# Per-head transposes of an attention gradient: from TensorE to the DMA crossbar, and the 1/rowsum multiply from GpSimd to VectorE

## Chip, cores, metric

One core of one Trainium2 chip (trn2). The metric is the device time of one execution in microseconds; lower is better. Between the executions of one kernel the time moves by some tenths of a per cent, in pin_both by 0.8%.

## The reference

The kernel computes the output and eight gradients of a block with a residual: `x + attention(layernorm(x)) * silu(gated_mlp(B_x))`. What matters here is the attention and its backward pass: 32 heads, 2048 queries and 2048 keys, head size 128, model width 576, bf16.

```python
def _A_ref(x, k_cache, v_cache, wq, wo):
    B, Sq, D = x.shape                       # 1, 2048, 576
    H, Dh = 32, 128
    q = (x @ wq).reshape(B, Sq, H, Dh).transpose(0, 2, 1, 3)
    scores = jnp.einsum("bhqd,bhkd->bhqk", q, k_cache) * (Dh ** -0.5)
    p = _softmax(scores, axis=-1)
    o = jnp.einsum("bhqk,bhkd->bhqd", p, v_cache)
    return o.transpose(0, 2, 1, 3).reshape(B, Sq, H * Dh) @ wo
# ... x + s * g, then jax.vjp of the whole for x, K, V, wq, wo and the three MLP weights
```

## The kernel before

Each head takes 32 steps, which I call slots. Slots 0 to 15 are pass 1, one row tile of 128 queries each: scores `sp` (TensorE), `exp` into a slab `Pq` (ScalarE), row sums and their reciprocals `rinv_all` (VectorE), and a transpose of the whole slab, `PT<-Pq`, by the DMA crossbar (the path on which a DMA transposes while it copies), 512 KB each. Five slots later `acc<-Vn,PT` uses PT. Slots 16 to 31 are pass 2: `dp`, then `Pq<-t,Pq` and `Pq<-dp,..` (VectorE), another crossbar transpose `dST<-Pq`, and five slots later `acc<-Kn,dST`. Between them lie the partial products for dV (`acc<-dOn,Pq`) and dK (`acc<-Qn,Pq`), which are staged in `kvo` and stored. So the crossbar already moves 32 x 512 KB per head, all issued from SyncE (SP).

Each head also needs its small operands in two layouts. Before the change TensorE makes them, in blocks of 128x128, and VectorE or ScalarE copies them out of PSUM, the memory that TensorE writes its results to:

```python
def pe_transpose_blocks(src_fn, lo, hi, dst_fn, eng):
    for g in range(lo, hi, 8):
        n = min(8, hi - g)
        pt = acc_tile(bf)                    # one of 4 PSUM buffers shared with every acc
        for j in range(n):
            nc.tensor.transpose(pt[:, j, :], src_fn(g + j), ident[:])
        alt.copy(dst_fn(g, n), pt[:, :n, :], eng=eng)

def prep_kt(hs):                             # prep_vt, prep_qn, prep_don, prep_wot: likewise
    KTv = hs.KT[:].rearrange("p (t q) -> p t q", q=P)
    pe_transpose_blocks(lambda j: hs.Kn[:, j, :], 0, NT, lambda g, n: KTv[:, g:g + n, :], "s")
# ...
def transpose_slab(hs, qt, name):            # the crossbar transposes of PT and dST
    T = wpt.tile([P, NT, P], bf, name=name, tag="PT")
    nc.sync.dma_start_transpose(T[:], hs.slabs[qt][:])
    return T
```

GpSimd multiplies dO and Q by 1/rowsum, and negates `delta`:

```python
def scale_don(hs, qt):
    nc.gpsimd.tensor_scalar(hs.dOn[:, qt, :], hs.dOn[:, qt, :], hs.rinv_all[:, qt:qt + 1], None, op0=ALU.mult)
# tail1, after acc<-Vn,PT of one row tile:
    nc.vector.scalar_tensor_tensor(junk[:], op_[:, 0, :], 1.0, hs.dOn[:, qt, :], op0=ALU.mult, op1=ALU.mult,
                                   accum_out=hs.delta[:, qt:qt + 1])
    nc.gpsimd.tensor_scalar(hs.negdelta[:, qt:qt + 1], hs.delta[:, qt:qt + 1], -1.0, None, op0=ALU.mult)
def post1(hs):                               # once, as pass 2 starts
    nc.gpsimd.tensor_scalar(hs.rsc[:], hs.rinv_all[:], SCALE, None, op0=ALU.mult)
    nc.gpsimd.tensor_tensor(hs.Qn[:], hs.Qn[:], hs.rsc[:].unsqueeze(2).to_broadcast([P, NT, P]), op=ALU.mult)
# main2:
    nc.scalar.activation(t[:], dp[:], AF.Identity, bias=hs.negdelta[:, qt:qt + 1], scale=1.0)
    nc.vector.tensor_tensor(Pq[:, hsl], t[:], Pq[:, hsl], op=ALU.mult)
# Partial.step, second half of dK or dV:
    fo_ = stg.tile([P, 4, P], bf, name="kvo")            # stg: two buffers
    nc.vector.tensor_tensor(fo_[...], self.tile[...], self.part[...], op=ALU.add)
    nc.gpsimd.dma_start(self.out_dram..., fo_[...])
# plan(h): which slot each piece is put at, in the program text (b1: slot 0 of the head, b2: slot 16)
    put(pl + q(skew + 3), NT * P, lambda: prep_kt(hd()))              # slot 24 of the head before
    put(b1 + q(sc + 1), nb * P, lambda sc=sc: prep_don(hd(), sc))     # slots 1..4
    put(b1 + qt + 1, 0, lambda qt=qt: scale_don(hd(), qt))
    put(b1 + q(NSC + 2), NT * P, lambda: prep_vt(hd()))               # slot 6
    put(b1 + q(NTH + 2), NT * P, lambda: prep_qn(hd()))               # slot 10
    put(b2 + 1, 0, lambda: post1(hd()))
```

## Time and profile before

| | before |
|---|---|
| time, median | 5353.21 us (3 executions) |
| attention stretch | 535 to 3731 us of the span |
| one head (mean of heads 4 to 27) | 100.2 us |

The first view is the top of the page of before: busy time and instructions of each engine, the DMA queues (packets, MB, share of 16 engines), and the chain that ended last by engine. The queue called hardware_dynamic is SyncE's, with the crossbar; software_dynamic is GpSimd's.

```profile
PE 5067.8 (95%) x54343; PEld 3653.5 (68%) x55220; DVE 2540.5 (48%) x5776; ACT 2649.6 (50%) x4710; POOL 1415.3 (26%) x2361
...
q1 hardware_dynamic: 2637890, 764.83, 71.7%
q0 software_dynamic: 83296, 280.64, 15.7%
...
PE 82%; issue 4%; DMA 2%; DVE 2%; SPq 2%; ACT 1%; POOL 1%; ACTq 0%; DVEq 0%; POOLq 0%
```

The second view takes 1000 to 3000 us of before (attention only): busy us of PE, PEld, DVE, ACT and POOL with instruction counts, then the granted clock, the DMA share and GB/s.

```profile
1000.00:3000.00 2000.00, 1932.53 (x24756) 1548.01 (x25153) 1167.44 (x2615) 1331.67 (x2256) 636.90 (x1097) 1.00 1.04 204
```

TensorE is busy 97% of this stretch. The DMA engines' share is 1.04. It can pass 1 because it adds up packets that overlap on one engine.

The waits of before, in us in total, times, and longest us:

```profile
ACT t L590 <- POOL negdelta L572: 175.8, 95, 3.0
PE dp L583 <- DVE Pq L586: 75.3, 78, 5.5
DVE kvo L627 <- DMA out_dram<-kvo: 23.6, 14, 6.1
```

For PT or dST, the crossbar's slab transposes, TensorE doesn't wait at all in before. One group of the page (busy us, mean ns of one, then idle time before it with its releaser):

```profile
L591 DVE TENSOR_TENSOR Pq<-t,Pq 128x1024 bf16<-128x1024 bf16 x512 | 422.6, 825 | 369.9 <-ACT t L590 366.4
```

The timeline of before, around one start of pass 2 (start us, us, engine, line, operation, tiles, and in brackets the idle time before it with its releaser):

```profile
1588.29 0.69 DVE L591 TENSOR_TENSOR Pq<-t,Pq 128x1024 bf16<-128x1024 bf16 x1 [0.69 <-ACT t L590]
...
1589.17 3.61 POOL L577 TENSOR_TENSOR Qn<-Qn,rsc 128x2048 bf16<-128x2048 bf16 x1
...
1590.49 2.84 DVE L591 TENSOR_TENSOR Pq<-t,Pq 128x1024 bf16<-128x1024 bf16 x1
...
1592.76 0.65 POOL L572 TENSOR_SCALAR negdelta<-delta 128x1 f32<-128x1 f32 x1
...
1594.79 0.38 PE L583 MATMUL dp<-VT,dOT 128*128 128x512 bf16 x1 [1.54 <-DVE Pq L586]
```

The same VectorE instruction takes 0.69 us alone and 2.84 us beside GpSimd's large multiply; then TensorE idles 1.54 us for it. The Trainium skill, page "SBUF — State Buffer", section "SBUF: two separate sides", describes a shared port pair of VectorE and GpSimd that is "an exclusive lock, not a bandwidth split". The 2.15 us of extra time agrees with that: the VectorE instruction ends at 1593.33 us, 0.55 us after GpSimd's.

### The profile page before, as it was taken

What the parts mean: (1) busy time and instruction counts of PE and PEld (TensorE: products, weight loads), DVE (VectorE), ACT (ScalarE), POOL (GpSimd) and SP (SyncE); (2) the same over time, 40 slices, a digit from 0 to 9 for tenths busy, and PEclk for the clock granted to TensorE, in tenths of its full rate; (3) what the DMA queues carried; (4) which work ended last, traced back from release to release, by engine and by line L of the source; (5) the groups of instructions that cost most, each with busy time, mean ns of one, the idle gap of its engine ahead of it and who ended that gap; (6) DMA issues with size and microseconds to landing.
All of it is one profiled execution on the core that took longest, in us unless ns stands there. A gap on an engine that the chain in (4) does not pass through costs nothing.

```text
span 5343.5 us, 129930 instructions
## 1 busy us (share of the span) xinstructions
PE 5067.8 (95%) x54343; PEld 3653.5 (68%) x55220; DVE 2540.5 (48%) x5776; ACT 2649.6 (50%) x4710; POOL 1415.3 (26%) x2361
## 2 busy tenths in 40 slices
PE   8899999999999999999999999999689999898999
PEld 3345777777777777777777777777457777544454
DVE  5644565566566566556566566566233333210011
ACT  7641766666666666666666666666222222100000
POOL 2122332332332332332332332332112232111000
PEclk9999999999999999999999999999899999999999
DMA  8767999999999999999999999999754455764875
GB/s 301 281 210 169 208 201 197 201 204 208 196 206 208 204 200 207 196 204 209 200 204 207 200 205 208 203 203 201 219 178 165 168 185 180 208 198 125 164 148 109
DMA packets 2721787, 1053.94 MB, mean 197 GB/s; under 512 B 2521937, under 2 KB 2642386, under 8 KB 2719138
## 3 DMA queue, kind: packets, MB, share of 16 engines
q1 hardware_dynamic: 2637890, 764.83, 71.7%
q0 software_dynamic: 83296, 280.64, 15.7%
q8 instruction: 433, 7.09, 0.6%
q14 instruction: 168, 1.38, 0.1%
HBM read 213.91 MB, written 201.00 MB: 78 GB/s over the span
## 4 chain that ended last, share of the span: by engine, by line
PE 82%; issue 4%; DMA 2%; DVE 2%; SPq 2%; ACT 1%; POOL 1%; ACTq 0%; DVEq 0%; POOLq 0%
PE acc L618 16%; PE acc L558 15%; PE acc L913 7%; PE sp L514 7%; PE accw L841 6%; PE dp L583 6%; PE acc L223 5%; PE dh L818 3%; PE accq L881 3%; PE acc L872 2%; PE acct L176 2%; PE acc L439 2%; PE accd L830 2%; PE acc L780 2%; DMA out_dram<-kvo 2%
## 5 line engine op out<-in xcount | busy, mean ns | idle before, releaser
L532 ACT ACTIVATE Pq<-sp 128x1024 bf16<-128x1024 f32 x1024 | 1047.0, 1023 | 307.8 <-PE sp L514 193.6
L618 PEld LDWEIGHTS <-Pq 128*128 128x128 bf16 x16384 | 1002.2, 98 | 240.4 <-issue 0.6
L590 ACT ACTIVATE t<-dp,negdelta 128x1024 bf16<-128x1024 f32 x512 | 571.1, 1115 | 283.3 <-POOL negdelta L572 175.8
L586 DVE SCALAR_TENSOR_TENSOR Pq<-dp,delta,Pq 128x1024 bf16<-128x1024 f32 x512 | 655.1, 1279 | 34.0 <-PE acc L558 32.0
L583 PE MATMUL dp<-VT,dOT 128*128 128x512 bf16 x1728 | 540.4, 379 | 75.8 <-DVE Pq L586 75.3
L591 DVE TENSOR_TENSOR Pq<-t,Pq 128x1024 bf16<-128x1024 bf16 x512 | 422.6, 825 | 369.9 <-ACT t L590 366.4
L558 PEld LDWEIGHTS <-PT 128*128 128x128 bf16 x8192 | 501.9, 98 | 121.6 <-issue 0.3
L618 PE MATMUL acc<-dOn,Pq 128*128 128x128 bf16 x8192 | 546.2, 219 | 10.1
L558 PE MATMUL acc<-Kn,dST 128*128 128x128 bf16 x8192 | 551.4, 219 | 3.6
L558 PE MATMUL acc<-Vn,PT 128*128 128x128 bf16 x8192 | 546.7, 219 | 7.0
L514 PE MATMUL sp<-KT,QT 128*128 128x512 bf16 x1762 | 547.1, 379 | 1.9 <-ACT Pq L532 1.9
L618 PE MATMUL acc<-Qn,Pq 128*128 128x128 bf16 x8192 | 541.5, 219 | 3.4
L558 PEld LDWEIGHTS <-dST 128*128 128x128 bf16 x8192 | 492.5, 98 | 61.2
L547 POOL TENSOR_SCALAR dOn<-dOn,rinv_all 128x128 bf16<-128x128 bf16 x512 | 312.6, 611 | 612.3 <-DVE rinv_all L520 495.4
L600 ACT ACTIVATE dq_n<-acc,rsc 128x128 bf16<-128x128 f32 x512 | 188.1, 367 | 326.1 <-PE acc L558 326.1
L841 PEld LDWEIGHTS <-xn_all 128*128 128x128 bf16 (+1 forms) x2880 | 281.5, 100 | 40.3 <-issue 11.1
L50 DVE TENSOR_SCALAR o_n<-acc,rinv_all 128x128 bf16<-128x128 f32 x352 | 123.5, 351 | 278.4 <-PE acc L558 277.7
L628 POOL DMA_DIRECT2D out_dram<-kvo x256 | 148.4, 580 | 394.8 <-DVE kvo L627 392.4
L583 PEld LDWEIGHTS <-dOT 128*128 128x128 bf16 x2048 | 164.9, 98 | 108.0 <-issue 85.8
L922 ACT ACTIVATE dxn<-acc 128x512 f32<-128x512 f32 (+1 forms) x32 | 12.7, 411 | 421.2 <-PE acc L913 421.2
L519 DVE TENSOR_REDUCE rs_all<-rsp 128x1 f32<-128x2 f32 x512 | 78.2, 153 | 291.9 <-ACT Pq L532 289.6
L552 POOL DMA_DIRECT2D dq_d<-dq_n x128 | 97.9, 765 | 441.4 <-ACT dq_n L600 431.0
(188 smaller groups left out, 7257.5 us busy)
## 6 DMA issues: line engine op xcount, KB each, us to landing
out_dram<-kvo POOLq DMA_DIRECT2D x256, 128.0 KB, 4.3
h_d<-h_row POOLq DMA_DIRECT2D x48, 384.0 KB, 4.1
a_d<-a_row POOLq DMA_DIRECT2D x48, 384.0 KB, 3.9
b_d<-b_row POOLq DMA_DIRECT2D x48, 384.0 KB, 4.6
a_blk<-a_d SPq DMA_DIRECT2D x18, 1024.0 KB, 5.8
b_blk<-b_d SPq DMA_DIRECT2D x18, 1024.0 KB, 18.7
h_blk<-h_d POOLq DMA_DIRECT2D x18, 1024.0 KB, 11.6
du_d<-du_blk POOLq DMA_DIRECT2D x18, 1024.0 KB, 9.1
```

Of the source, the lines that this page charges most:

```text
L223: nc.tensor.matmul(av[:, :CH], lhsT=w[:kk, i, :], rhs=srcT[:kk, i, cs], start=(i == 0), stop=(i == DT - 1))
L514: nc.tensor.matmul(sp[:, c * CH:(c + 1) * CH], lhsT=hs.QT[:, qt * P:(qt + 1) * P], rhs=hs.KT[:, hf * HW_ + c * CH: hf * HW_ + (c + 1) * CH ...
L532: nc.scalar.activation(Pq[:, hsl], sp[:], AF.Exp, scale=SCALE, accum_out=hs.rsp[:, hf:hf + 1])
L547: nc.gpsimd.tensor_scalar(hs.dOn[:, qt, :], hs.dOn[:, qt, :], hs.rinv_all[:, qt:qt + 1], None, op0=ALU.mult)
L558: nc.tensor.matmul(hs.acc[:, 0, :], lhsT=T[:, kt, :], rhs=rhs[:, kt, :], start=(kt == 0), stop=(kt == NT - 1))
L583: nc.tensor.matmul(dp[:, c * CH:(c + 1) * CH], lhsT=hs.dOT[:, qt * P:(qt + 1) * P], rhs=hs.VT[:, hf * HW_ + c * CH: hf * HW_ + (c + 1) * C ...
L586: nc.vector.scalar_tensor_tensor(Pq[:, hsl], dp[:], hs.delta[:, qt:qt + 1], Pq[:, hsl], op0=ALU.subtract, op1=ALU.mult)
L590: nc.scalar.activation(t[:], dp[:], AF.Identity, bias=hs.negdelta[:, qt:qt + 1], scale=1.0)
L591: nc.vector.tensor_tensor(Pq[:, hsl], t[:], Pq[:, hsl], op=ALU.mult)
L618: nc.tensor.matmul(self.tile[:, j, :], lhsT=self.slabs[qt][:, kt * P:(kt + 1) * P], rhs=self.rhs[:, qt, :], start=(qt == self.lo), stop=(q ...
L841: nc.tensor.matmul(acc[:kd, :], lhsT=xn_all[:, st, d0:d0 + kd], rhs=blk_[:, st, :], start=(st == 0), stop=(st == NT - 1))
L913: nc.tensor.matmul(accs[sl][j][:, :nn], lhsT=ch[:, kk, sl * P:(sl + 1) * P], rhs=wT[:, k0 + kk, n0:n0 + nn], start=(kidx == 0), stop=(kidx ...
```

## The change

Its intent: the transposes need no TensorE time if the crossbar does them; and if VectorE multiplies by 1/rowsum in one row tile at a time, GpSimd holds no port against it. The core of the diff (loads, padding of `wo_h` to five full blocks, and signatures are cut):

```diff
 def prep_kt(hs):
-    pe_transpose_blocks(lambda j: hs.Kn[:, j, :], 0, NT, lambda g, n: KTv[:, g:g + n, :], "s")
+    nc.sync.dma_start_transpose(hs.KT[:].rearrange("p (t q) -> p t q", q=P), hs.Kn[:].rearrange("p t d -> p (t d)"))
 # prep_vt and prep_wot likewise
 def prep_don(hs, sc):
-    pe_transpose_blocks(lambda j: hs.dOT[:, j * P:(j + 1) * P], sc * nb, (sc + 1) * nb, ...)
+    nc.sync.dma_start_transpose(hs.dOn[:, sc * nb:(sc + 1) * nb, :], hs.dOT[:, sc * CH:(sc + 1) * CH])
 def prep_qn(hs):
-    pe_transpose_blocks(lambda j: hs.QT[:, j * P:(j + 1) * P], 0, NT, ...)
+    nc.sync.dma_start_transpose(hs.Qn[:], hs.QT[:])
 ...
 def scale_don(hs, qt):
-    nc.gpsimd.tensor_scalar(hs.dOn[:, qt, :], ...)
+    nc.vector.tensor_scalar(hs.dOn[:, qt, :], ...)
+def scale_qn(hs, qt):
+    nc.vector.tensor_scalar(hs.Qn[:, qt, :], hs.Qn[:, qt, :], hs.rinv_all[:, qt:qt + 1], None, op0=ALU.mult)
 ...
-    nc.vector.scalar_tensor_tensor(junk[:], op_[:, 0, :], 1.0, hs.dOn[:, qt, :], ..., accum_out=hs.delta[:, qt:qt + 1])
-    nc.gpsimd.tensor_scalar(hs.negdelta[:, qt:qt + 1], hs.delta[:, qt:qt + 1], -1.0, None, op0=ALU.mult)
+    nc.vector.scalar_tensor_tensor(junk[:], op_[:, 0, :], -1.0, hs.dOn[:, qt, :], ..., accum_out=hs.negdelta[:, qt:qt + 1])
 def post1(hs):
-    nc.gpsimd.tensor_scalar(hs.rsc[:], hs.rinv_all[:], SCALE, None, op0=ALU.mult)
-    nc.gpsimd.tensor_tensor(hs.Qn[:], hs.Qn[:], hs.rsc[:].unsqueeze(2).to_broadcast([P, NT, P]), op=ALU.mult)
+    nc.vector.tensor_scalar(hs.rsc[:], hs.rinv_all[:], SCALE, None, op0=ALU.mult)
 # main2: the last half adds negdelta where it subtracted delta
 # Partial: SCALE is now the factor of the dK copies (scalar_tensor_tensor with factor, mult and add)
 ...
-    put(b1 + qt + 1, 0, lambda qt=qt: scale_don(hd(), qt))
+    put(b1 + max(qt + 1, q(4 + qt // nb)), 0, lambda qt=qt: scale_don(hd(), qt))
-    put(b1 + q(NTH + 2), NT * P, lambda: prep_qn(hd()))
+    put(b1 + q(NTH + 1), 0, lambda: prep_qn(hd()))                    # slot 9
+    for qt in range(NT):
+        put(max(b1 + qt + 1, b1 + NT - 4 + qt // 2), 0, lambda qt=qt: scale_qn(hd(), qt))   # slots 12..19
```

More of the change, by code (lines that the diff above doesn't have):

```diff
@@ L169, in acc_tile @@
         return acc_box[0](dtype)
-    def pe_transpose_blocks(src_fn, lo, hi, dst_fn, eng):
-        for g in range(lo, hi, 8):
-            n = min(8, hi - g)
-            pt = acc_tile(bf)
-            for j in range(n):
-                nc.tensor.transpose(pt[:, j, :], src_fn(g + j), ident[:])
-            alt.copy(dst_fn(g, n), pt[:, :n, :], eng=eng)
     class HeadState:
@@ L191, in prep_loads @@
             nc.gpsimd.dma_start(hs.wq[:kd_last, nf, :], A_wq[nf * P:, hcols])
-        nc.gpsimd.dma_start(wo_h[:], A_wo[hcols, :])
+        nc.gpsimd.dma_start(wo_h[:, :D], A_wo[hcols, :])
         hs.Kn = Kns[h % 2]
@@ L199, in prep_kt @@
     def prep_kt(hs):
-        KTv = hs.KT[:].rearrange("p (t q) -> p t q", q=P)
-        pe_transpose_blocks(lambda j: hs.Kn[:, j, :], 0, NT, lambda g, n: KTv[:, g:g + n, :], "s")
+        nc.sync.dma_start_transpose(hs.KT[:].rearrange("p (t q) -> p t q", q=P), hs.Kn[:].rearrange("p t d -> p (t d)"))
     def prep_vt(hs):
-        VTv = hs.VT[:].rearrange("p (t q) -> p t q", q=P)
-        pe_transpose_blocks(lambda j: hs.Vn[:, j, :], 0, NT, lambda g, n: VTv[:, g:g + n, :], "v")
+        nc.sync.dma_start_transpose(hs.VT[:].rearrange("p (t q) -> p t q", q=P), hs.Vn[:].rearrange("p t d -> p (t d)"))
     def prep_wot(hs):
-        pt = acc_tile(bf)
-        for i, (d0, kd) in enumerate(dts):
-            nc.tensor.transpose(pt[:kd, i, :], wo_h[:, d0:d0 + kd], ident[:])
-        nf = DT - 1 if KPAD else DT
-        if nf:
-            alt.copy(hs.woT[:, :nf, :], pt[:, :nf, :], eng="s")
-        if KPAD:
-            alt.copy(hs.woT[:kd_last, nf, :], pt[:kd_last, nf, :], eng="s")
+        nc.sync.dma_start_transpose(hs.woT[:], wo_h[:])
     def gen_T(w, srcT, dst, sc, eng):
@@ L232, in prep_don @@
     def prep_don(hs, sc):
-        pe_transpose_blocks(lambda j: hs.dOT[:, j * P:(j + 1) * P], sc * nb, (sc + 1) * nb,
-                            lambda g, n: hs.dOn[:, g:g + n, :], "v")
+        nc.sync.dma_start_transpose(hs.dOn[:, sc * nb:(sc + 1) * nb, :], hs.dOT[:, sc * CH:(sc + 1) * CH])
     def prep_qn(hs):
-        pe_transpose_blocks(lambda j: hs.QT[:, j * P:(j + 1) * P], 0, NT, lambda g, n: hs.Qn[:, g:g + n, :], "v")
+        nc.sync.dma_start_transpose(hs.Qn[:], hs.QT[:])
     px = tc.alloc_tile_pool(name="px", bufs=1)
@@ L404 @@
         woTs = [pdT.tile([P, DT, P], bf, name=f"woT_h{b}") for b in range(2)]
-        for t_ in wqs + woTs:
+        for t_ in wqs:
             zpad(t_)
-        wo_h = pdT.tile([P, D], bf, name="wo_h")
+        wo_h = pdT.tile([P, DT * P], bf, name="wo_h")
+        if KPAD:
+            nc.gpsimd.memset(wo_h[:, D:], 0.0)
         Kns = [pdT.tile([P, NT, P], bf, name=f"Kn{b}") for b in range(2)]
@@ L497, in start_head @@
                 hs.rinv_all = hstat.tile([P, NT], f32, name="rinv_all")
-                hs.delta = hstat.tile([P, NT], f32, name="delta")
                 hs.negdelta = hstat.tile([P, NT], f32, name="negdelta")
@@ L546, in scale_don @@
             def scale_don(hs, qt):
-                nc.gpsimd.tensor_scalar(hs.dOn[:, qt, :], hs.dOn[:, qt, :], hs.rinv_all[:, qt:qt + 1], None, op0=ALU.mult)
+                nc.vector.tensor_scalar(hs.dOn[:, qt, :], hs.dOn[:, qt, :], hs.rinv_all[:, qt:qt + 1], None, op0=ALU.mult)
+            def scale_qn(hs, qt):
+                nc.vector.tensor_scalar(hs.Qn[:, qt, :], hs.Qn[:, qt, :], hs.rinv_all[:, qt:qt + 1], None, op0=ALU.mult)
             def store_nat(hs, buf, qt, dst_d):
@@ L569, in tail1 @@
                 junk = wt.tile([P, P], f32, name="junk")
-                nc.vector.scalar_tensor_tensor(junk[:], op_[:, 0, :], 1.0, hs.dOn[:, qt, :], op0=ALU.mult, op1=ALU.mult,
-                                               accum_out=hs.delta[:, qt:qt + 1])
-                nc.gpsimd.tensor_scalar(hs.negdelta[:, qt:qt + 1], hs.delta[:, qt:qt + 1], -1.0, None, op0=ALU.mult)
+                nc.vector.scalar_tensor_tensor(junk[:], op_[:, 0, :], -1.0, hs.dOn[:, qt, :], op0=ALU.mult, op1=ALU.mult,
+                                               accum_out=hs.negdelta[:, qt:qt + 1])
                 store_nat(hs, hs.o_n, qt, on2_d)
             def post1(hs):
-                nc.gpsimd.tensor_scalar(hs.rsc[:], hs.rinv_all[:], SCALE, None, op0=ALU.mult)
-                nc.gpsimd.tensor_tensor(hs.Qn[:], hs.Qn[:], hs.rsc[:].unsqueeze(2).to_broadcast([P, NT, P]), op=ALU.mult)
+                nc.vector.tensor_scalar(hs.rsc[:], hs.rinv_all[:], SCALE, None, op0=ALU.mult)
             def main2(hs, qt, hf):
@@ L585, in main2 @@
                 if hf == NHF - 1:
-                    nc.vector.scalar_tensor_tensor(Pq[:, hsl], dp[:], hs.delta[:, qt:qt + 1], Pq[:, hsl], op0=ALU.subtract, op1=ALU.mult)
+                    nc.vector.scalar_tensor_tensor(Pq[:, hsl], dp[:], hs.negdelta[:, qt:qt + 1], Pq[:, hsl], op0=ALU.add, op1=ALU.mult)
                     hs.dST[qt] = transpose_slab(hs, qt, "dST")
@@ L603, in attention, with __init__ @@
             class Partial:
-                def __init__(self, hs, lo, hi, rhs, part, out_dram, eng):
+                def __init__(self, hs, lo, hi, rhs, part, out_dram, eng, factor=1.0):
+                    self.factor = factor
                     self.lo, self.hi, self.rhs = lo, hi, rhs
@@ L623, in step @@
                         if self.out_dram is None:
-                            alt.copy(self.part[:, k0:kt + 1, :], self.tile[:, :j + 1, :], eng=self.eng)
+                            if self.factor == 1.0:
+                                alt.copy(self.part[:, k0:kt + 1, :], self.tile[:, :j + 1, :], eng=self.eng)
+                            else:
+                                alt.scaled(self.part[:, k0:kt + 1, :], self.tile[:, :j + 1, :], self.factor, eng=self.eng)
                         else:
                             fo_ = stg.tile([P, 4, P], bf, name="kvo")
-                            nc.vector.tensor_tensor(fo_[:, :j + 1, :], self.tile[:, :j + 1, :], self.part[:, k0:kt + 1, :], op=ALU.add)
+                            nc.vector.scalar_tensor_tensor(fo_[:, :j + 1, :], self.tile[:, :j + 1, :], self.factor, self.part[:, k0:kt + 1, :],
+                                                           op0=ALU.mult, op1=ALU.add)
                             nc.gpsimd.dma_start(self.out_dram.rearrange("(p t) d -> p t d", t=NT)[:, k0:kt + 1, :], fo_[:, :j + 1, :])
@@ L664, in plan @@
                     put(pl + q(skew + 1), 0, lambda: heads.__setitem__(h, start_head(h)))
-                    put(pl + q(skew + 3), NT * P, lambda: prep_kt(hd()))
-                    put(pl + q(skew + 4), DT * P, lambda: prep_wot(hd()))
+                    put(pl + q(skew + 3), 0, lambda: prep_kt(hd()))
+                    put(pl + q(skew + 4), 0, lambda: prep_wot(hd()))
                     for sc in range(NSC):
@@ L673, in plan, with first @@
                     put(b1 + q(sc), DT * CH, lambda sc=sc: prep_dot(hd(), sc))
-                    put(b1 + q(sc + 1), nb * P, lambda sc=sc: prep_don(hd(), sc))
+                    put(b1 + q(sc + 1), 0, lambda sc=sc: prep_don(hd(), sc))
                 for qt in range(NT):
-                    put(b1 + qt + 1, 0, lambda qt=qt: scale_don(hd(), qt))
-                put(b1 + q(NSC + 2), NT * P, lambda: prep_vt(hd()))
-                put(b1 + q(NTH + 2), NT * P, lambda: prep_qn(hd()))
+                    put(b1 + max(qt + 1, q(4 + qt // nb)), 0, lambda qt=qt: scale_don(hd(), qt))
+                put(b1 + q(NSC + 2), 0, lambda: prep_vt(hd()))
+                put(b1 + q(NTH + 1), 0, lambda: prep_qn(hd()))
+                for qt in range(NT):
+                    put(max(b1 + qt + 1, b1 + NT - 4 + qt // 2), 0, lambda qt=qt: scale_qn(hd(), qt))
                 put(b2 + 1, 0, lambda: post1(hd()))
                 parts = {}
-                def first(key, rhs, lo, hi, eng):
+                def first(key, rhs, lo, hi, eng, factor=1.0):
                     parts[key] = part_tile()
-                    return Partial(hd(), lo, hi, rhs, parts[key], None, eng)
+                    return Partial(hd(), lo, hi, rhs, parts[key], None, eng, factor)
                 spread(b1 + NTH, lambda: first("v", hd().dOn, 0, NTH, "v"))
                 spread(b2, lambda: Partial(hd(), NTH, NT, hd().dOn, parts["v"], out_3[0, h], None))
-                spread(b2 + NTH, lambda: first("k", hd().Qn, 0, NTH, "s"))
-                spread(b2 + NT, lambda: Partial(hd(), NTH, NT, hd().Qn, parts["k"], out_2[0, h], None))
+                spread(b2 + NTH, lambda: first("k", hd().Qn, 0, NTH, "s", SCALE))
+                spread(b2 + NT, lambda: Partial(hd(), NTH, NT, hd().Qn, parts["k"], out_2[0, h], None, SCALE))
                 for qt in range(NT):
```

## The prediction

> **What bounds it now.** TensorE, in the attention stretch (530 to 3750 us, 32 heads of about 100 us). The table by stretches has TensorE matmuls busy 1932.5 of 2000 us between 1000 and 3000 us (97%), clock 1.00; ScalarE 67%, VectorE 58%, GpSimd 32%. The DMA engines look full (share 1.04), but that sum counts packets waiting on each other. The DMA records there move 256-byte transpose packets at 288 GB/s in the best 2 us, 167 GB/s on average: room, in bursts little.
>
> **What the change removes.**
> 1. 69 TensorE transposes per head (16 each of K, V, dO, Q; 5 of wo). From start to start they hold TensorE 17.9+17.9+17.8+17.8+9.9 us over 20 heads (the 219 ns shown for one is latency): 4.06 us per head, 130 us in all, all on the path.
> 2. GpSimd's multiply of Qn (one 128x2048 op, 3.61 us) right after pass 2 starts. The timeline of one head shows VectorE's Pq<-t,Pq taking 2.84 us instead of 0.69 beside it, negdelta queued behind it on GpSimd, and the chain of waits going through both: TensorE idles 0.30+1.54 us before dp. In the waits view "PE dp waits for DVE Pq" is 75 us, 2.3 us per head. The Trainium skill, "SBUF — State Buffer" (the shared port pair), says VectorE and GpSimd share a port pair by exclusive lock, the loser blocked for the whole instruction; the 2.15 us of blocking agrees. About 1.7 us per head goes, 55 us.
> 3. ScalarE and VectorE copies out of PSUM (2.9 and 4.4 us per head) and the negdelta hop: otherwise off the path.
>
> **What it adds.**
> - 4.3 transposes of 512 KB per head on a queue that does 32. At 1.8 us (burst) to 2.35 us (back to back) each: 8 to 10 us per head, total near 85 of 94 us. No throughput limit, but slots 4 to 12 of pass 1 (row tiles), where V and Q are added, are at the rate limit; PT lands up to 8.5 us after issue there and is used about 10 us after. Estimate 0.5 us of TensorE wait per head.
> - 32 VectorE multiplies of 128x128 bf16 per head, estimated 0.2 us each (small VectorE ops take 0.15 to 0.35 us), 6 us. In slots 16 to 24 VectorE is nearly as loaded as TensorE (about 20 of 21 us); eight Q multiplies fall there. Estimate 0.6 us per head given back.
>
> **Sum.** 5353 - 130 - 55 + 35 = 5203 us (-2.8%). Range 5150 to 5270. Faster by over 2% (under 5246): 0.77; within 2%: 0.21; slower by over 2%: 0.02.
>
> **What would show each step.** Right: head period near 95.5 us; no GpSimd arithmetic in attention; Pq<-t,Pq mean from 825 to about 700 ns; "dp waits for DVE Pq" from 75 to under 40 us; the transposes' queue from 765 to about 835 MB; stages before 530 and after 3750 us unchanged. Wrong: TensorE waiting before acc<-PT or acc<-dST, or for KT or woT; VectorE stalled on dOn or Qn landing; ScalarE's exp (2.43 us per slot) limiting pass 1 slots, which fall to 2.65 us of TensorE work or less.
>
> **What would make it wrong.** The SP queue is in order: a transpose of dO that waits for its VectorE copy, or of K for its load, holds all slab transposes behind it. If crossbar transposes beside GpSimd's stores slow to half rate (packets of over 100 ns are seen), TensorE waits for PT and the gain shrinks to under 2%.

## More of the kernel before

The instructions of each engine are put in a compiled order when the kernel is built, and in the traces an instruction can stand well ahead of its place in the text: in after, K's transpose for the next head is issued in about slot 15 where the text has it in slot 24.

## The result, and the profile after

| | before | after |
|---|---|---|
| time, median | 5352.11 us (5349.72 to 5353.54, 4 runs) | 5478.33 us (5474.73 to 5483.89, 4 runs) |
| ratio | | 1.0241 (95%: 1.0226 to 1.0255) |
| attention start / length / rest, us | 535 / 3196 / 1613 | 550 / 3320 / 1606 |
| one head (mean of heads 4 to 27) | 100.2 us | 104.2 us |

A ratio here is the mean time of one kernel's fast runs over that of the other's of the same rounds, so it is not quite the ratio of the medians quoted. The change is slower by 2.4%, its outputs are correct, and the difference lies in the attention stretch.

The page of after, the same parts:

```profile
PE 5071.7 (93%) x53012; PEld 3580.8 (65%) x53012; DVE 2520.8 (46%) x6576; ACT 2576.9 (47%) x4582; POOL 820.5 (15%) x1272
...
q1 hardware_dynamic: 2928706, 837.22, 77.7%
q0 software_dynamic: 83296, 280.64, 16.0%
...
PE 70%; DMA 11%; issue 7%; DVE 3%; SPq 2%; ACT 1%; POOL 1%; POOLq 0%; ACTq 0%; DVEq 0%
```

The chain that ended last gives the headline: TensorE's part fell from 82% to 70%, and DMA's rose from 2% to 11%. The kernel has begun to wait for transfers. The stretch from 1000 to 3000 us of after:

```profile
1000.00:3000.00 2000.00, 1852.99 (x22892) 1446.30 (x22890) 1112.81 (x3008) 1237.17 (x2094) 254.79 (x401) 0.97 1.13 217
```

TensorE is busy 1853 us instead of 1933 of 2000, and its clock there fell from 1.00 to 0.97. The waits of after:

```profile
DVE Qn L533 <- DMA Qn<-QT: 245.4, 32, 10.4
DVE dOn L530 <- DMA dOn<-dOT: 188.5, 32, 8.4
PE acc L544 <- DVE junk L556: 126.3, 31, 6.8
PE acc L206 <- DVE dOT L42: 49.1, 30, 3.9
PE acc L544 <- DMA dST<-Pq: 27.9, 15, 4.1
PE dp L567 <- DVE Pq L570: 26.9, 48, 3.6
PE acc L544 <- DMA PT<-Pq: 9.5, 13, 1.7
```

The last line but one is the wait that the change was to remove, and most of it went: 75.3 to 26.9 us. The first two are new. VectorE waits once in each of the 32 heads for the crossbar's Qn and once for its dOn, 434 us in all, and TensorE then waits for VectorE (lines 3 and 4). One group of after (busy us, mean ns, then idle time before it) shows the other thing that was predicted:

```profile
L575 DVE TENSOR_TENSOR Pq<-t,Pq 128x1024 bf16<-128x1024 bf16 x512 | 354.3, 692 | 317.1 <-ACT t L574 310.2
```

The mean of `Pq<-t,Pq` is 692 ns; in before the same group has 825. The timeline of after, in slot 11 of one head, shows how a multiply of 0.25 us costs 4.67 us:

```profile
1398.62 2.83 SPq L219 DMA_TRANSPOSE Qn<-QT  x1
...
1401.46 0.59 PE L497 MATMUL sp<-KT,QT 128*128 128x512 bf16 x2
...
1404.23 1.23 DVE L533 TENSOR_SCALAR Qn<-Qn,rinv_all 128x128 bf16<-128x128 bf16 x7 [8.19 <-DMA Qn<-QT]
...
1406.38 0.28 DVE L556 SCALAR_TENSOR_TENSOR junk<-acc,dOn 128x128 f32<-128x128 f32 x1
...
1406.72 1.87 PE L544 MATMUL acc<-Vn,PT 128*128 128x128 bf16 x16 [4.67 <-DVE junk L556]
```

Seven multiplies of Qn stand in VectorE's order in front of the `junk` that frees a PSUM buffer. The text has them in slots 12 to 15. The compiled order put them right behind the `junk` of row tile 5, in slot 10, before the crossbar had delivered Qn. VectorE, which runs in order, stood still for 8.19 us, the PSUM buffers of `acc` ran out, and TensorE stopped. After that stop its matmuls run slower: 16 of them take 1.87 us where they take 1.06 elsewhere. The records show a granted clock of 0.5 for 3.4 to 6.8 us after such a stop. The Trainium skill, page "TensorE: Matmul & The Clock Gate", section "Why this matters for your kernels", advises no idle gaps over about 3 us for that reason. The time lost to the half clock, each record's length times (1 - clock) summed over the attention stretch, is 3.4 us in before and 99.0 us in after.

Cut by slot (worked out from the starts of TensorE's instructions, mean of heads 4 to 27; "work" is the slot less its gaps):

```
slot     before: us  work   gap      after: us  work   gap
  2             3.95  3.74  0.22           5.69  3.73  1.96   dO copied from PSUM behind dOn multiplies
  6             3.54  3.54  0.00           2.65  2.65  0.00   16 transposes of V gone
 10             3.54  3.33  0.22           2.81  2.66  0.15   16 transposes of Q gone
 11             2.65  2.65  0.00           8.60  3.85  4.74   the stop shown above, and the slow clock
 18             4.35  2.43  1.91           2.65  2.65  0.00   GpSimd's large multiply gone
 24             3.61  2.88  0.73           3.35  2.26  1.08   dp and dST
```

Gaps of 0.22 us in before are matmul records missing from the trace, not waits. The gains came as predicted (slots 6, 10, 18); the losses are in slots 2 and 11 (1.74 and 5.95 us), with 0.34 and 0.39 us in slots 12 and 23. Slot 24 has a longer gap but is shorter as a whole.

### The profile page after: what moved, and what is told of

The parts are those of the page before. It is cut to its first block, busy times and chain, and to the rows that moved or that the text cites. A ratio compares the mean times of both kernels' runs of the same rounds, so it can differ in the third digit from the quotient of the medians.

```text
span 5476.1 us, 126347 instructions
## 1 busy us (share of the span) xinstructions
PE 5071.7 (93%) x53012; PEld 3580.8 (65%) x53012; DVE 2520.8 (46%) x6576; ACT 2576.9 (47%) x4582; POOL 820.5 (15%) x1272
## 4 chain that ended last, share of the span: by engine, by line
PE 70%; DMA 11%; issue 7%; DVE 3%; SPq 2%; ACT 1%; POOL 1%; POOLq 0%; ACTq 0%; DVEq 0%
PE acc L544 12%; PE acc L603 12%; PE acc L904 7%; PE sp L497 6%; PE dp L567 6%; PE accw L832 6%; PE acc L206 4%; PE dh L809 3%; DMA Qn<-QT 3%; PE accq L872 3%; PE acc L863 2%; PE accd L821 2%; PE acc L771 2%; DMA out_dram<-kvo 2%; DMA dOn<-dOT 2%
## 5 line engine op out<-in xcount | busy, mean ns | idle before, releaser
L603 PEld LDWEIGHTS <-Pq 128*128 128x128 bf16 x16384 | 1026.3, 99 | 251.6 <-issue 20.5
L570 DVE SCALAR_TENSOR_TENSOR Pq<-dp,negdelta,Pq 128x1024 bf16<-128x1024 f32 x512 | 655.5, 1280 | 55.9 <-PE dp L567 54.9
L567 PE MATMUL dp<-VT,dOT 128*128 128x512 bf16 x2048 | 612.9, 381 | 27.0 <-DVE Pq L570 26.9
L497 PE MATMUL sp<-KT,QT 128*128 128x512 bf16 x2048 | 631.3, 391 | 5.1 <-ACT Pq L515 4.9
L575 DVE TENSOR_TENSOR Pq<-t,Pq 128x1024 bf16<-128x1024 bf16 x512 | 354.3, 692 | 317.1 <-ACT t L574 310.2
L538 POOL DMA_DIRECT2D on_d<-o_n x128 | 96.8, 756 | 882.3 <-DVE junk L556 510.2
L530 DVE TENSOR_SCALAR dOn<-dOn,rinv_all 128x128 bf16<-128x128 bf16 x512 | 130.4, 255 | 205.6 <-DMA dOn<-dOT 188.5
L533 DVE TENSOR_SCALAR Qn<-Qn,rinv_all 128x128 bf16<-128x128 bf16 x512 | 110.7, 249 | 245.4 <-DMA Qn<-QT 245.4
L359 PE MATMUL g_ps<-wg_sb,xnT 128*128 128x512 bf16 x720 | 185.3, 388 | 33.0 <-ACT oma L365 26.1
L615 DVE SCALAR_TENSOR_TENSOR kvo<-acc,part 128x512 bf16<-128x512 f32 x256 | 175.6, 686 | 87.0 <-DMA out_dram<-kvo 36.6
```

Source lines behind the costliest of these rows:

```text
L497: nc.tensor.matmul(sp[:, c * CH:(c + 1) * CH], lhsT=hs.QT[:, qt * P:(qt + 1) * P], rhs=hs.KT[:, hf * HW_ + c * CH: hf * HW_ + (c + 1) * CH ...
L567: nc.tensor.matmul(dp[:, c * CH:(c + 1) * CH], lhsT=hs.dOT[:, qt * P:(qt + 1) * P], rhs=hs.VT[:, hf * HW_ + c * CH: hf * HW_ + (c + 1) * C ...
L570: nc.vector.scalar_tensor_tensor(Pq[:, hsl], dp[:], hs.negdelta[:, qt:qt + 1], Pq[:, hsl], op0=ALU.add, op1=ALU.mult)
L603: nc.tensor.matmul(self.tile[:, j, :], lhsT=self.slabs[qt][:, kt * P:(kt + 1) * P], rhs=self.rhs[:, qt, :], start=(qt == self.lo), stop=(q ...
```

## The experiments

Two theories stood at the start.

- A, order: the crossbar's load is harmless; the multiplies of dOn and Qn were put too early in VectorE's compiled order and stall it.
- B, load: the DMA engines had no room for 13% more crossbar bytes (16.78 to 19.05 MB per head); whatever the order, something waits for them.

Twelve kernels ran in four groups, each group on its own chip with its own runs of before: pin_both, pin_qn, extra and all_pe (before: 5351.7 us, median); nokv, spread, kvw and kvw4 (5347.68); k27, vw4 and all_pe4 (5347.06); all_pe4p (5353.95). Ratios are to before of the same group. All outputs are correct except where said.

### pin_both: the multiplies kept where the text has them

```diff
+            anchor[0] = nc.vector.reciprocal(hs.rinv_all[:, qt:qt + 1], ...)   # also the junk of tail1
 def scale_qn(hs, qt):                                                          # and scale_don
-    nc.vector.tensor_scalar(hs.Qn[:, qt, :], ...)
+    with tc.issue_after(anchor[0].ins):
+        nc.vector.tensor_scalar(hs.Qn[:, qt, :], ...)
```

Each multiply is ordered behind the last `rinv_all` or `junk` instruction of VectorE that stands before it in the text. Nothing else changes in the text; in the trace the transpose of K moved too, from slot 15 to slot 17.

> The changed kernel with one thing added: order edges (no waits) that keep the VectorE multiplies of Qn and dOn at the row tiles where the program text puts them (Qn from tile 12 of pass 1, dOn from tile 4), where the compiled order of the changed kernel has them about two and four tiles earlier. Theory A (VectorE, in order, sits at a multiply whose transpose has not landed, and TensorE runs out of PSUM tiles behind it): TensorE's idle time at tiles 2 and 11 of pass 1 (2.0 and 4.7 us per head, and 1.2 us of slow clock after it) goes, about 250 us: 5200 to 5270 us, and VectorE's waits for landings of Qn and dOn fall from 434 to under 80 us. Theory B (the crossbar transposes overload the DMA engines, and everything that needs a slab comes late): within 60 us of the changed kernel, over 5410 us, with the idle time moved to the matmuls that read PT and dST.

Measured: 5404.31 us, ratio 1.0089 (1.0062 to 1.0117). Between the two ranges, and only 6 us under B's. Order cost about 74 us, but with it mended the kernel is still slower than before. Its waits:

```profile
PE acc L547 <- DMA PT<-Pq: 160.7, 118, 5.7
PE acc L547 <- DMA dST<-Pq: 54.1, 48, 3.1
DVE dOn L532 <- DMA dOn<-dOT: 1.8, 1, 1.8
```

The wait for dOn is gone (188.5 to 1.8 us), that for Qn no longer appears among the largest, and slots 2 and 11 lost their gaps from it. In place of them TensorE now waits for the crossbar itself: 9.5 us for PT in after, 160.7 here. In after it probably was hidden behind the VectorE stop, during which the queue could catch up. TensorE's idle time hardly fell: counting gaps of over 150 ns, it is 7.6 us per head in after and 7.3 in pin_both. What fell is the rest, from 96.7 to 95.2 us per head, with the records of the half clock: 32.4 us in place of 99.0, as many short waits took the place of a few long stops. (pin_both's traced execution, 5432.13 us, is the slowest of its four, so the traces differ by 46 us and not by 74.)

### pin_qn: only the multiplies of Qn kept in place

The same edit for `scale_qn` alone.

> The same order edges for Qn alone. Theory A: the idle time at tile 11 goes and that at tile 2 (dOn, 2.0 us per head) stays: 5478 - 6 x 32 = 5285 us, 5260 to 5330. Theory B: over 5410 us.

Measured: 5433.88 us, 1.0154 (1.0134 to 1.0175), in B's range and far from A's. VectorE still waits 210.1 us for dOn. So of the 74 us that order cost, the Qn part is about 44 us and the dOn part about 30 us (differences of the medians).

### extra: before, with the same crossbar load added and nothing else

```diff
 def prep_vt(hs):                                   # likewise in prep_kt, prep_wot, prep_don, prep_qn
+    nc.sync.dma_start_transpose(scr[0][:], hs.Vn[:].rearrange("p t d -> p (t d)"))
     pe_transpose_blocks(...)                       # still there
```

The transposes of the change, almost the same bytes (four blocks of wo instead of five), go into a scratch tile that nothing reads. TensorE and GpSimd still do all of their work.

> The kernel before, TensorE transposes kept, plus the change's crossbar transposes of K, V, dO, Q and wo at the same places into a scratch tile that nobody reads (72 MB more, output right). It has the added DMA load without the added dependences. Theory A: load alone costs little, 5340 to 5410 us (at most 1% over before). Theory B: it costs as much as the change lost against what it saved, 5480 us or more.

Measured: 5545.69 us, 1.0369 (1.035 to 1.0388): 194 us slower than before, 6.1 us per head. It is in B's range. This is the decisive run: load alone costs more than the 185 us that the change was to gain. All of it lies in slots 6 to 15 of pass 1, which take 6.1 us more per head than in before; the other 22 slots together take the same time. Its waits:

```profile
PE acc L567 <- DMA PT<-Pq: 147.2, 107, 3.9
PE dp L592 <- DVE Pq L595: 71.6, 77, 1.9
```

TensorE waits for PT, and GpSimd's wait is where it was. Since one scratch tile takes them all, the SP queue must sometimes wait for the transpose before; those waits are 32 us in all, so they may account for a small part of the 194 but not for most.

### all_pe: the change with every transpose back on TensorE

```diff
-    nc.sync.dma_start_transpose(hs.Qn[:], hs.QT[:])      # and K, V, dO, wo
+    pe_transpose_blocks(lambda j: hs.QT[:, j * P:(j + 1) * P], 0, NT, lambda g, n: hs.Qn[:, g:g + n, :], "v")
```

This leaves only the move from GpSimd to VectorE.

> The changed kernel with all transposes back on TensorE: what is left is the scaling on VectorE, negdelta made directly, and GpSimd free of arithmetic. If step 2 of the prediction (the GpSimd multiply blocks VectorE, 1.7 us per head) is right: 5285 to 5320 us, and the mean of Pq<-t,Pq is 690 to 700 ns. If it is wrong: 5340 us or more. Both theories agree here.

Measured: 5347.2 us, 0.9987 (0.9967 to 1.0008). A miss: about 50 us were expected and nearly none came. Slot 18 is 1.7 us shorter (4.35 to 2.65), so the mechanism holds, but two losses hide it. First, slot 24 now takes 4.81 us per head (3.61 in before), behind VectorE's wait for the stores of dV and dK, which the waits view shows (23.6 us in before):

```profile
DVE kvo L629 <- DMA out_dram<-kvo: 60.1, 23, 11.4
```

Second, the part after attention is 20 us longer (1633 against 1613). That is of my own making and not of the change: the copies there alternate between VectorE and ScalarE by a counter that runs through the whole program, the edit left it odd, and all copies of that stage changed engines.

### all_pe4 and all_pe4p: those two losses taken away

all_pe4 gives the store staging four buffers; all_pe4p sets the counter back as well.

```diff
-    fo_ = stg.tile([P, 4, P], bf, name="kvo")
+    fo_ = stg.tile([P, 4, P], bf, name="kvo", bufs=4)
 # all_pe4p only, after attention:
+    alt.i += 1
```

> all_pe with 4 staging buffers for the dK and dV stores. all_pe gained 5 us instead of the 55 us of step 2: the idle time at slots 17 and 18 was gone (1.7 us per head), and 1.0 us per head came back at slot 24, behind VectorE's wait for those stores. If that is where it went: 5295 to 5325 us. If it is lost elsewhere: 5335 to 5350.

> all_pe4 with one count added to the switch that alternates PSUM copies between VectorE and ScalarE, after attention. all_pe and all_pe4 make an odd number of switched copies fewer, so in the stage after attention the two engines' copies were swapped against the kernel before, and that stage took about 20 us longer in both their traces (1632 us after the last attention slot, 1605 to 1613 in every other trace), while attention itself was 27 and 63 us shorter. If that swap is the rest: 5280 to 5295 us, and the stretch after attention is back at about 1610 us. If not: 5300 to 5315 us.

Measured: all_pe4 5307.62 us, 0.9926 (0.991 to 0.9941), the gap of slot 24 down to 0.4 us; all_pe4p 5292.95 us, 0.9887 (0.9862 to 0.9912), with the last part back at 1608 us. Both are as expected. So taking the multiplies off GpSimd was worth about what was predicted: slots 17 and 18 are 1.76 us shorter per head than in before, 56 us over the 32 heads, and the attention stretch of all_pe4p is 53 us shorter (3143 against 3196). The edit also takes away the hop of `negdelta` through GpSimd, and no run separates the two; the timeline of before shows TensorE's 1.54 us behind the blocked VectorE. What four buffers alone would do for before was not run; its wait for those stores is 23.6 us in all, so at most about that.

### nokv: does less other DMA traffic help?

pin_both without six of the eight stores of dV and dK per head; two outputs are wrong.

```diff
-                            nc.gpsimd.dma_start(self.out_dram..., fo_[...])
+                            if k0 == 0:
+                                nc.gpsimd.dma_start(self.out_dram..., fo_[...])
```

> pin_both with 6 of the 8 stores of dK and dV per head left out (wrong on purpose: three quarters of two outputs unwritten). TensorE, VectorE and ScalarE do the same work. In pin_both the DMA records have the engines moving bytes, or holding a crossbar packet with no byte moving, for 99 of 102.5 us per head. Theory B (DMA engines full): 0.79 MB per head less, 3 us of copying and perhaps 3 us of held packets: the head falls to 97 to 99 us, 5404 - 110 to 180: 5225 to 5295 us. Theory A (VectorE waiting for landings in order): 5370 us or more, since its order is the same.

Measured: 5310.99 us, 0.9936 (0.9916 to 0.9957). With 0.78 MB less per head, through another queue, issued by another engine, the kernel is 93 us faster than pin_both by the medians (two chips; the ratios to before say 1.5%). It is nearer to B's range than to A's but outside both. TensorE's waits for the crossbar, 160.7 and 54.1 us in pin_both, fall by 100 us in all, which is about the gain, while VectorE's wait for those stores was only 20.1 us in pin_both:

```profile
PE acc L547 <- DMA PT<-Pq: 79.7, 81, 4.5
PE acc L547 <- DMA dST<-Pq: 35.2, 38, 2.8
```

The Trainium skill, page "DMA: Bandwidth & Descriptors", section "Issuing engines are not separate DMA queues", says that transfers run on the same 16 DMA engines whoever starts them, and this run agrees with it. Part of what I expected failed: the time in which packets are held (below) did not fall with the stores: 13.7 us per head in pin_both, 14.0 here.

### spread: the transposes of K and Q moved out of pass 1

pin_both with K's and Q's transposes ordered behind the last PT of pass 1, and the Q multiplies at slots 20 to 23.

```diff
-    put(b1 + q(NTH + 1), 0, lambda: prep_qn(hd()))
+    put(b2, 0, lambda: behind(prep_qn, hd()))          # behind: with tc.issue_after(lastPT[0].ins)
-    put(max(b1 + qt + 1, b1 + NT - 4 + qt // 2), 0, lambda qt=qt: scale_qn(hd(), qt))
+    put(b2 + 4 + qt // 4, 0, lambda qt=qt: scale_qn(hd(), qt))
```

> pin_both with the same bytes, but the crossbar transposes of K and Q ordered behind the last PT of pass 1, so that they run at tiles 16 to 18, where the DMA engines of the kernel before were busy 11.1 of 15 us, instead of at tiles 5 to 12, where they were busy 97%; the multiplies of Qn go to tiles 20 to 23. If the loss is local crowding in pass 1: the waits for PT at tiles 8 to 13 (5 us per head) go, 5240 to 5310 us. If the total is what is short (99 us of DMA work per head): 5340 to 5400 us, with waits for dST in pass 2 instead.

Measured: 5431.93 us, 1.0156 (1.013 to 1.0182), above both ranges and worse than pin_both. TensorE's wait for PT fell, but that for dST rose:

```profile
PE acc L550 <- DMA dST<-Pq: 129.6, 34, 7.5
PE acc L550 <- DMA PT<-Pq: 45.8, 41, 3.5
```

In slot 21 alone TensorE waits 4.1 us for dST, and the time lost to the half clock in attention is 81.9 us (32.4 in pin_both). In the traced executions the attention stretch is as long as in pin_both (3271 and 3269 us): the crowding moved from pass 1 to pass 2. So pass 1 is not the only place where the transposes don't fit. Whether the total or the new place is to blame, this run doesn't tell; k27 below speaks for the place.

### kvw and kvw4: dO and Q back on TensorE

```diff
 # prep_don and prep_qn as in before; K, V and wo on the crossbar, K ordered behind the last PT; kvw4: kvo bufs=4
+    put(pl + q(skew + 3), 0, lambda: behind(prep_kt, hd()))
```

> The changed kernel with dO and Q back on TensorE (no VectorE multiply waits for a landing any more), K, V and wo kept on the crossbar, K ordered behind the last PT of pass 1. DMA work per head estimated at 85.4 + 2.3 x 3.2 = 93 us, TensorE at 96 us: 5352 - 73 (37 transposes per head) - 5 (what all_pe gained) = 5275, 5250 to 5310 us. Theory A and B agree that it beats before; if it is 5340 us or more, even a load below saturation costs what it saves.

> kvw with 4 staging buffers for the dK and dV stores instead of 2. In all_pe VectorE waited 60 us for such stores to land (24 us before) and TensorE idled 1.7 us per head at tile 24 behind it. If that is where the gain of step 2 went: 20 to 40 us under kvw. If not: within 10 us of kvw.

Measured: kvw 5292.46 us, 0.9892 (0.9876 to 0.9909), as expected; kvw4 5279.44 us, 0.9872 (0.9847 to 0.9898), 13 us under kvw and in neither range. Those intervals overlap, so here the four buffers are not shown to help. Both beat before. The two operands whose transposes VectorE had to wait for, and half of the added bytes, are off the queue.

### k27 and vw4: less, or later

k27 is kvw4 with K's transpose ordered behind the dST of row tile 11 of pass 2, so that it falls in slots 28 to 31. There the DMA engines were taken for only 10.3 of 13.2 us in before, by the count of the next section; in k27 it is 13.0 of 13.3. vw4 leaves only V and wo on the crossbar.

```diff
 # k27, in transpose_slab:
+    if name == "dST" and qt == NT - 5:
+        lastPT[0] = last
-    put(pl + q(skew + 3), 0, lambda: behind(prep_kt, hd()))
+    put(pl + NT - 4, 0, lambda: behind(prep_kt, hd()))
```

> kvw4 with the crossbar transpose of K ordered behind the dS transpose of row tile 11 of pass 2 (tile slot 27), not behind the last PT (slot 16). In kvw4 TensorE still idles 2.1 us per head at slots 22 to 24 for dST, where the DMA engines have no free time; in the kernel before they had 3 us free at slots 28 to 31. If lateness comes from where the added transposes fall: those waits shrink to about 0.5 us per head, 5225 to 5255 us. If only the total counts: within 10 us of kvw4 (5279).

> kvw4 with K back on TensorE too; only V and wo stay on the crossbar. TensorE gets 0.9 us per head more, the DMA engines 3 us less. If the DMA engines cost kvw4 its 2.1 us per head of dST waits: 5279 + 28 - 50 = about 5255, 5240 to 5275 us. If not: 5300 to 5315.

Measured: k27 5254.8 us, 0.9828 (0.9812 to 0.9845); vw4 5260.66 us, 0.9837 (0.9819 to 0.9855). They can't be told apart. vw4 is where it was expected if the DMA engines cost kvw4 its waits, and k27 at the upper edge of the range for "lateness comes from where the added transposes fall". k27 moves the same bytes as kvw4 and is 25 us faster by the medians (two chips; 0.4% by the ratios, whose intervals just miss each other), so the place of an added transpose seems to count and not the total alone. k27's waits show what is left:

```profile
PE acc L556 <- DMA dST<-Pq: 30.3, 16, 8.7
PE acc L556 <- DMA PT<-Pq: 6.3, 10, 1.6
```

### Where the DMA engines' time goes

From the DMA records of heads 4 to 27 I marked each 0.1 us by what happened in it: bytes moved by SyncE's queue only (nearly all crossbar), by GpSimd's only, by both; nothing moved but a crossbar packet of over 200 ns was open ("held"); or none of these ("idle"). Us per head; the bin and the thresholds are mine, so the sums are a measure for comparing these kernels and not an absolute.

```
kernel     head  SyncE  GpSimd  both   held   sum of these   idle   MB of SyncE's queue
before    100.2   62.9     7.6   3.6   11.3           85.4   15.0       16.78
extra     106.3   72.8     7.4   4.3   12.8           97.3    9.2       19.01
after     104.2   72.6     6.9   4.9   12.8           97.2    7.6       19.05
pin_both  102.5   73.2     6.9   5.5   13.7           99.3    3.7       19.05
nokv       99.6   73.0     5.4   4.0   14.0           96.4    3.4       19.03
kvw4       98.1   68.2     6.9   5.2   12.7           93.0    5.5       17.99
k27        97.1   68.3     6.4   5.4   14.2           94.3    3.2       17.96
vw4        97.4   65.8     7.2   4.6   13.2           90.8    7.3       17.48
all_pe     99.6   63.1     7.3   4.1   12.5           87.0   13.0       16.78
```

In pin_both the DMA engines are taken for 99 of 102.5 us while TensorE needs about 95. So what bounds the head there is no longer TensorE. In slots 6 to 15 of before they were already taken for 28.1 of 28.7 us: added bytes could not fit there; in extra it is 33.7 of 34.9 us, and that stretch holds the whole loss of extra, although 9.2 us of the head are idle elsewhere.

SyncE, which issues the transposes one after another, is a rival: its records of DMA_TRANSPOSE fill 74.1 us of a head in before and 98.0 in pin_both. That is 2.3 and 2.7 us per 512 KB, and the shortest took 1.4 us, so the length is not fixed. In nokv, with the same transposes and fewer stores by GpSimd, it is 95.1 us: the issue gets longer with what the DMA engines carry. This speaks for the engines as the limit, but no run separates the two fully.

The change added 2.27 MB and, in pin_both, 13.9 us. While only SyncE's queue moves, it moves 249 to 258 GB/s by this count, in every kernel; so the added bytes met a rate, and no slowdown of that rate is seen. The Trainium skill, page "DMA: Bandwidth & Descriptors", section "Latency and other measured facts", gives 261 GB/s for a transpose with a non-contiguous middle dimension and about 350 to 400 for the contiguous case. The rate here is within 5% of the first; no run shows which of the two cases these transposes are.

## Why the prediction was wrong, point by point

1. **TensorE's transposes, 4.06 us per head: right where it can be read.** Slots 6 and 10 fell from 3.54 to 2.65 and 2.81 us, slot 1 from 3.95 to 3.73, slot 25 (wo) from 4.07 to 3.76; in slot 6 that is 16 times 55.8 ns.
2. **GpSimd's lock, 55 us: right in mechanism, and in size where it acted.** `Pq<-t,Pq` fell from 825 to 692 ns (about 700 predicted), "dp waits for DVE Pq" from 75.3 to 26.9 us (under 40 predicted). Slots 17 and 18 gave 56 us in all_pe. In the whole kernel all_pe4p shows 53 us in the attention stretch once four store buffers take away what hid it; some of that, about 24 us at most, could be the buffers' own. Without them almost nothing is gained, since VectorE then waits for stores.
3. **The crossbar, "8 to 10 us per head, total near 85 of 94 us. No throughput limit": the step that failed.** The total was 85.4 before anything was added. I had counted the slab transposes (about 75 us at 2.35 us each) and left out GpSimd's transfers on the same engines, 7.6 us alone and 3.6 us beside the crossbar, and the 11 us in which packets are held. The added transposes took 11.9 us (extra) to 13.9 us (pin_both) more than before; against all_pe, which does the same other work without them (87.0 us), pin_both took 12.3 us more. That is 2.8 to 3.2 us for 512 KB and not 1.8 to 2.35. The sum is 99 of a head that was to be 95.5 us long. That the predicted total, 85, is what before already had is chance. The prediction had even put slots 4 to 12 at the rate limit, and still gave them half a microsecond; in extra slots 6 to 15 cost 6.1 us. In place of "0.5 us of TensorE wait per head", TensorE waits 5.0 us for PT and 1.7 us for dST in pin_both (160.7 and 54.1 us over 32 heads), and load alone costs 194 us in extra. I had the DMA share of 1.04 in view and set it aside because packets overlap in that sum. That was a reason not to read it as 104%, and no reason to read it as "room".
4. **VectorE's multiplies, "estimated 0.2 us each": right in size, wrong in kind.** They take 0.25 us. Their cost is where they stand. I reasoned with the slots of the text; the compiled order put seven Qn multiplies in slot 10 and the first dOn multiplies in slot 1. That cost about 74 us (after to pin_both), by the traces mostly through the half clock after each long stop: TensorE's idle time is nearly the same in both, 7.6 and 7.3 us per head. "VectorE stalled on dOn or Qn landing" was named as a sign of being wrong, and it came; its size was not in the sum.
5. **Stages outside: nearly right.** Attention begins 15 us later and the rest is 7 us shorter.

The sum, from the runs: before 5352; TensorE's transposes and GpSimd's lock, 185 us by the prediction; load, about +194 (extra); order, about +74 (after to pin_both). 5352 - 185 + 194 + 74 = 5435, 43 us below the 5478 measured. The terms are not independent: in pin_both the crossbar's transfers bound the head, so there TensorE's saving buys little. I don't split the 43 us further.

Where the saving ends is shown by the partial versions. V and wo together are 21 of the 69 transposes, 1.24 us of TensorE per head by their share of 4.06, or 40 us in all. vw4 (5260.66) lies 32 us under all_pe4p (5292.95), on another chip: nearly all of it is gained, with 7.3 us of idle DMA time left. K is 16 more, 30 us by the same count. k27 gains 6 us over vw4, within the error, and idle falls to 3.2 us. Adding dO and Q turns it into a loss.

The version to keep is k27, or vw4, which is simpler: VectorE's multiplies, four store buffers, dO and Q (and in vw4 also K) on TensorE. k27 is 1.7% faster than before and, dividing the two ratios (0.9828 / 1.0241), 4.0% faster than the change. The Trainium skill, page "VectorE: DVE Perf Modes", section "Rules for kernel authors", says in one line: "Use TensorE if PSUM dest is OK; xbar DMA otherwise". For dO and Q this case agrees; for V and wo it does not, since vw4 is faster than all_pe4p. TensorE takes 55.8 ns from one 128x128 transpose to the next, the crossbar 147 ns per block where slab transposes are issued back to back (2.35 us for 16, the median in pin_both).

Still open: how much of the limit is the DMA engines and how much SyncE's issue; what holds the crossbar's packets, 11 to 14 us per head in every kernel, nokv included; and what four buffers alone would give before.

## What to carry to other kernels

Before moving work to the DMA engines, add up what they already do in the stretch where it will fall: every queue that shares them, and the time in which nothing moves but something is pending. A busy share above 1 is a question to be taken apart, not a number to be dismissed. And when a transfer replaces a step that made its consumer wait on nothing, look at where the compiled order puts the consumer; a 0.25 us instruction at the wrong place of an in-order engine can stop the engine that bounds the kernel, and the clock after it.

## What the Trainium skill lacked or had wrong

- No page has the held crossbar packets: some 15 to 19 times per head and DMA engine a 256-byte packet stays open over 0.2 us, mostly 0.3 to 1.7 us, against a median of 18 ns, and in 11 to 14 us per head nothing moves at all. With it in the count, an added 512 KB transpose cost 2.8 to 3.2 us here, beside all other transfers, which is 164 to 187 GB/s, less than the 261 GB/s or 350 to 400 GB/s of "DMA: Bandwidth & Descriptors" ("Latency and other measured facts"). While only SyncE's queue moves, 249 to 258 GB/s are near the 261.
- "VectorE: DVE Perf Modes" ("The three transpose paths") gives 390 ns for a 128x128 transpose on TensorE and 1309 ns on the crossbar. In streams these are 55.8 ns from start to start and 147 ns here, so neither figure of that table tells what a kernel pays, and their ratio is 2.6 and not 3.4.
- No page says that the DMA share of a profile can pass 1 (1.04 here with 15 us of a 100 us head idle), or how to read it.
